# Products of a tile of ones in the planned TensorE gaps of the first batch's attention

## The chip, the cores and the metric
One NeuronCore of one Trainium2 chip runs the whole program. The metric is the time of one execution on the device, in microseconds (us); lower is better. Engines are named as in the profile: PE is TensorE's matmul stream and PEld its weight loads, DVE is VectorE, ACT is ScalarE, POOL is GpSimd, SP issues the transfers. Each engine runs its instructions in the order in which the program gives them, and waits on semaphores where an operand comes from, or a buffer is still read by, another engine.

## What is computed
Attention with rotary embedding over 4 batches, 8 heads, 576 positions and 64 columns a head, and then a gated layer over all 2304 rows:

```python
scores = matmul(rotate(q), rotate(k).T) / sqrt(64)
attn   = exp(scores - max(scores)); attn /= sum(attn) + 1e-9
x      = (attn @ v)  laid out as (2304, 512)
gate   = 1 / (1 + exp(-(x @ w_gate)))            # w_gate, w_val: 512 x 1536
out    = (gate * (x @ w_val)) @ w_out            # w_out: 1536 x 512
```

## The kernel before
**Tiling.** The heads are worked on in 4 pairs (`p`), one head in each half of the 128 partitions. The queries of a pair are split in two halves (`i`) of 256 and 320 columns. The first batch (b = 0) has a path of its own, in fp32. Its generator `front` (lines 626 to 668) makes the scores of a block of 128 queries in one PSUM tile `s` (line 641; the "direct" products) and takes their maximum over the keys on DVE (line 645, a read of both banks of `s`). After the blocks of a half, five short DVE steps (lines 652 to 656) split the maxima in three bf16 parts, PE turns them (line 661), and ACT copies them out (line 668). `back` (lines 670 to 722) then makes the scores the other way round, keys on partitions: products of a tile of ones `onesb` with the negated maxima (line 685) plus the scores (line 690) accumulate in `s`, ACT takes the exponential (line 696), and PE makes the weighted sums `pv` and the row sums `m` (line 707), which DVE divides (lines 717 and 718).

**Beside it.** While batch 0's attention runs, the weights come in: ACT and DVE decode and scale twelve chunks (lines 372 to 400), with a small product per chunk on PE (line 349). From some 93 us on, the gated layer of batch 0 (line 799) begins and PE has work from it between the attention's tasks. Batches 1 to 3 and the last layer (line 833) follow.

**PSUM.** `s_ps` are two tiles of 128 x 2 x 512 fp32, each two banks; the direct products and their readers use columns 0 to 287 of each bank, the others columns 0 to 255 or 319. Columns 384 to 511 of the second bank are written and read by nobody. `v_ps` is one bank, of which the weighted sums use columns 0 to 319 and small maxima (lines 337 to 342) use columns from 384. `m_ps` are three more banks.

**Order.** Every piece of work is a task with an engine, an estimated cost, a rank, and the buffers that it reads and writes. `Plan.order` plays the tasks through with these costs and gives each a planned start; `Plan.emit` then issues the instructions in the order of the planned starts, so each engine's queue has the planner's order. The planner's times decide the order alone: on the chip nothing waits for a planned time. The waits come from the Tile framework, which follows each access to a tile and puts a semaphore wait on the later of two that clash. In PSUM it counts accesses to one bank of a tile as a clash, whatever their columns: in the program of this kernel, the first weighted sums after `values` of a batch (writes of columns 0 to 255 of `pv`) wait for the DVE instruction of line 324 that reads column 384 of that bank and nothing else of `pv`.

Of the kernel before, what the change touches and what calls it, by code (L numbers as in the profile page):

```python
# [35 lines left out]
class Lease:  # L36


    def __init__(self, pool, bufs):
        self.pool, self.bufs, self.users, self.n = pool, bufs, [], None  # L40
# [18 lines left out]
class Plan:  # L59


    HOP = 0.2

    def __init__(self):
        self.tasks, self.preds, self.wrote, self.read = [], [], {}, {}
# [26 lines left out]
    def order(self):  # L92
# [34 lines left out]
        def release(n):  # L127
            for x in self.leases[n]:
                x.left -= 1
                if not x.left:  # L130
                    slots[x.pool][x.n] = max(done[m][1] + done[m][2] for m in x.users) + self.HOP
                    for m in parked.pop(x.pool, []):
                        offer(m)

        def offer(n):
            for e, _ in self.tasks[n][0]:
                t = 0.0
                for m in self.preds[n]:
                    e0, end, land = done[m]
                    t = max(t, end if e0 == e and not land else end + land + self.HOP)  # L140
                heapq.heappush(wait.setdefault(e, []), (t, self.tasks[n][1], n))
# [60 lines left out]

    def emit(self):
        self.starts = self.order()
        for t, n, e in self.starts:
            self.tasks[n][2](e)


# [17 lines left out]
def rope_attention_then_sigmoid_glu(ctx: ExitStack, tc: tile.TileContext, qk, v, w_in, w_out, tables, out):  # L226
    nc = tc.nc
    V, A, G, T, Y = nc.vector, nc.scalar, nc.gpsimd, nc.tensor, nc.sync
# [47 lines left out]
    onesb = sb("onesb", [128, 128], BF16)  # L276
# [4 lines left out]
    s_ps = [psum.tile([128, 2, 512], F32, name=f"s{n}") for n in range(2)]  # L281
# [3 lines left out]
    P = Plan()  # L285
# [628 lines left out]
    for f in range(NF):  # L914
        t = -1.75 + 0.35 * f / NF
        at(t, w_in_chunk, f, t)
    hiddens(0, 0, -1.6, -1.2)
    for f in range(NF):
        t = -1.0 + 0.2 * f / NF
# [14 lines left out]
        projects(b, 1, b + 0.8, b + 1)  # L934
    for _, _, fn, args in sorted(todo):
        fn(*args)
    with tc.manual_schedule():
        P.emit()
    global LAST
# [46 lines left out]
```

## Time and profile before
| | |
|---|---|
| median of 3 runs | 716.72 us (716.29 to 717.3) |
| span of the profiled execution | 719.6 us; its own time is known by this span alone |
| PE busy | 672.3 us (93%), 4986 products |
| DVE busy | 482.9 us (67%) |
| ACT busy | 437.0 us (61%) |
| mean granted TensorE clock | 0.974 of full speed |
| chain that ended last | PE 85%, DVE 8%, ACT 3%, DMA 2% |

Busy times are sums over an engine's instructions. The page also cuts the span into 40 slices of 18 us; the first five or six are the first batch's attention, where PE's busy share is lowest. Idle time of an engine matters only where the chain that ended last runs through it.

### The profile page before, as it was taken

Reading aid. Unit: us, or ns where it says so; the run is one execution under the profiler, and the core shown is the slowest. Engines: PE = TensorE matmul, PEld = TensorE weight load, DVE = VectorE, ACT = ScalarE, POOL = GpSimd, SP = SyncE. Lnnn points to the kernel's source line nnn. Section 1 sums busy time; section 2 is a strip of 40 time slices with the busy share of each in tenths; the row PEclk is TensorE's granted clock in tenths of the full one; section 3 lists DMA queues with packets and bytes.
Section 4 is the critical chain, followed back from the end, with each engine's and each line's share of the span. In section 5 each row is a group of like instructions: output and inputs, shape, how many; then the busy total and the mean of one; then the engine's idle time right before and its main releaser. Section 6 shows DMA issues by size and latency. Waiting matters only on the chain.

```text
span 719.6 us, 12869 instructions
## 1 busy us (share of the span) xinstructions
PE 672.3 (93%) x4986; PEld 426.9 (59%) x4986; DVE 482.9 (67%) x1062; ACT 437.0 (61%) x885; POOL 73.9 (10%) x57
## 2 busy tenths in 40 slices
PE   1687889999999998998998899999999999999997
PEld 1343455565675455775564665578667756866753
DVE  5677676889888668877797886779938682311310
ACT  2583967796878866665776678577738663322320
POOL 0300000000303001133135001114000000000000
PEclk9996989999999999999998999999999999999999
DMA  9731305226364337664996559764544542000001
GB/s 348 315 125 62 133 41 209 93 92 215 122 163 99 96 96 178 161 165 87 203 210 142 105 126 231 166 159 118 126 110 117 90 109 79 1 15 16 1 15 30
DMA packets 145230, 89.38 MB, mean 124 GB/s; under 512 B 128912, under 2 KB 133648, under 8 KB 143248
## 3 DMA queue, kind: packets, MB, share of 16 engines
q1 hardware_dynamic: 145168, 88.56, 45.7%
q8 instruction: 39, 0.64, 0.4%
q14 instruction: 23, 0.19, 0.1%
HBM read 43.12 MB, written 4.72 MB: 66 GB/s over the span
## 4 chain that ended last, share of the span: by engine, by line
PE 85%; DVE 8%; ACT 3%; DMA 2%; issue 1%; SPq 0%; DVEq 0%; ACTq 0%
PE m L799 37%; PE m L833 20%; PE pv L748 6%; PE s L584 5%; PE s L641 3%; PE s L572 3%; PE pv L707 3%; PE s L690 2%; PE m L707 2%; DVE p L366 1%; PE s L685 1%; DVE p L607 1%; DMA stk<-in_qk_dram 1%; DMA pt<-p 1%; DVE m L645 1%
## 5 line engine op out<-in xcount | busy, mean ns | idle before, releaser
L799 PE MATMUL m<-xt,w 128*128 128x320 f16 (+1 forms) x2304 | 297.1, 287 | 2.3 <-ACT th L805 2.3
L799 PEld LDWEIGHTS <-w 128*128 128x128 f16 x2304 | 221.7, 98 | 74.3 <-issue 18.6
L833 PE MATMUL m<-wo,gt 128*128 128x512 f16 x648 | 146.4, 381 | 0.0
L612 ACT ACTIVATE p<-p,st 128x576 f32<-128x576 f32 x108 | 83.1, 770 | 52.0 <-DVE p L607 45.3
L833 PEld LDWEIGHTS <-gt 128*128 128x128 f16 x648 | 62.4, 98 | 74.2 <-issue 5.0
L366 DVE SCALAR_TENSOR_TENSOR p<-p,st,p 128x576 f16<-128x576 f32 x108 | 91.5, 874 | 20.5 <-ACT p L360 20.2
L809 DVE SCALAR_TENSOR_TENSOR th<-th,m 128x256 f32<-128x256 f32 (+1 forms) x96 | 43.1, 450 | 75.1 <-PE m L799 71.9
L360 ACT ACTIVATE p<-p,st 128x576 f16<-128x576 f32 x108 | 78.3, 763 | 10.6 <-DMA pt<-p 4.5
L360 ACT ACTIVATE gt<-th,c_s 128x256 f16<-128x256 f32 (+1 forms) x96 | 50.5, 529 | 55.2 <-DVE th L809 54.9
L366 DVE SCALAR_TENSOR_TENSOR gt<-th,c_s,gt 128x256 f16<-128x256 f32 (+1 forms) x96 | 56.0, 589 | 19.6 <-ACT gt L360 19.4
L805 ACT ACTIVATE th<-m,gsc 128x256 f32<-128x256 f32 (+1 forms) x96 | 47.3, 494 | 35.1 <-PE m L799 34.5
L607 DVE TENSOR_SCALAR_CACHE_REDUCE p<-s,q_e 128x576 f32<-128x576 f32 x72 | 57.2, 811 | 4.7 <-PE s L584 3.9
L748 PE MATMUL pv<-pt,v 128*64 128x256 f16 (+3 forms) x720 | 54.3, 299 | 0.0
L584 PE MATMUL s<-stk 128*128 128x288 f16 (+1 forms) x320 | 44.9, 290 | 6.4 <-DVE p L607 6.4
L641 PE MATMUL s<-stk 64*128 64x288 f32 (+1 forms) x160 | 33.5, 527 | 18.5 <-DVE stk L516 12.3
L523 POOL TENSOR_TENSOR sw<-sw,tab 128x576 f32<-128x576 f32 x16 | 25.7, 1606 | 225.1 <-DMA sw<-in_qk_dram 225.1
L748 PEld LDWEIGHTS <-v 128*64 128x64 f16 (+1 forms) x720 | 37.3, 113 | 17.6 <-issue 12.8
L521 POOL TENSOR_TENSOR qk<-qk,tab 128x576 f32<-128x576 f32 x16 | 22.8, 1446 | 203.9 <-DMA qk<-in_qk_dram 152.2
L584 PEld LDWEIGHTS <-stk 128*128 128x128 f16 (+1 forms) x320 | 27.2, 100 | 20.0 <-issue 11.9
L645 DVE TENSOR_REDUCE m<-s 128x2 f32<-128x576 f32 x36 | 26.9, 753 | 15.1 <-PE s L641 14.7
L360 ACT ACTIVATE o<-m,o_s 128x512 f32<-128x512 f32 x16 | 10.9, 682 | 41.0 <-PE m L833 40.9
L696 ACT ACTIVATE pt<-s 128x512 f32<-128x512 f32 (+3 forms) x40 | 23.8, 601 | 15.5 <-PE s L690 15.3
(122 smaller groups left out, 700.0 us busy)
## 6 DMA issues: line engine op xcount, KB each, us to landing
wo<-in_w_dram SPq DMA_DIRECT2D x12, 1024.0 KB, 4.8
sw<-in_qk_dram SPq DMA_DIRECT2D x16, 576.0 KB, 5.0
xt<-in_wo_dram SPq DMA_DIRECT2D x12, 512.0 KB, 4.5
stk<-in_qk_dram SPq DMA_DIRECT2D x8, 576.0 KB, 5.0
qk<-in_qk_dram SPq DMA_DIRECT2D x8, 576.0 KB, 5.6
out_dram<-o SPq DMA_DIRECT2D x16, 256.0 KB, 2.1
xt<-in_v_dram SPq DMA_DIRECT2D x3, 1152.0 KB, 6.2
stk<-sw SPq DMA_DIRECT2D x16, 216.0 KB, 3.2
```

The lines of the kernel that those rows point to most:

```text
L360: A.activation(o, src, AF.Copy, scale=scale)
L366: V.scalar_tensor_tensor(out=o, in0=src, scalar=scale, in1=hi, op0=ALU.mult, op1=ALU.subtract)
L584: T.matmul(o[:, c, 0:288], lhsT=q[:, rows:rows + width], rhs=kk[:, c * 288:c * 288 + 288], start=(m == 0), stop=(m == 1))
L607: lambda E, h=h, c=c: V.tensor_scalar(out=prs[c]().rearrange("p (c n) -> p c n", c=2), in0=h()[:, :, 0:288], scalar1=down, scalar2=None, o ...
L612: lambda E, c=c: A.activation(prs[c](), prs[c](), AF.Exp, bias=st[:, k, 0, c:c + 1], scale=-1.0, accum_out=st[:, k, 1, c:c + 1]))
L641: T.matmul(o, lhsT=qT[hs, 128 * t:128 * t + w], rhs=kT[hs, 288 * cc:288 * cc + 288], start=True, stop=True)
L707: T.matmul(o[es, 0:n], lhsT=ones[hs, 0:64] if one else v32[hs, p, j if j == 4 else j + 5 * e], rhs=pp[hs, at0:at0 + n], start=(j == 0), st ...
L748: T.matmul(v_ps[64 * e:64 * e + 64, 0:n], lhsT=v16[hs, p, a, g, :], rhs=pt[z][hs, c * 9 + g, 0:n], start=(first and m == 0), stop=(last an ...
L799: T.matmul(m()[:, 0:n], lhsT=w16[:, f, g, a, cc, :], rhs=x[:, cc, c, c0:c0 + n], start=(k == 0), stop=(k == 11))
L805: op("ACT", c_act(n), rank - 0.05, [m, ("gsc", b, f)], [r], lambda E, m=m: A.activation(t(), m()[:, 0:n], AF.Tanh, scale=gsc[:, b, f:f + 1]))
L809: op("DVE", c_dve(n, psum=True), rank - 0.05, [m], [r], lambda E, m=m: V.scalar_tensor_tensor(out=t(), in0=t(), scalar=1.0, in1=m()[:, 0:n ...
L833: T.matmul(m(), lhsT=gt[:, f, a, c0:c0 + 128], rhs=wo16[:, f, c, :], start=(f == 0 and k == 0), stop=(f == NF - 1 and k == 2))
```

## The change
`emit` keeps the planned end `last` of the PE task before. Ahead of each PE task it issues fillers: for a planned gap of g us between two PE tasks, `int((g - 0.3) * 8)` of them, and for the gap ahead of the first PE task, counted from 1.5 us, `int((g - 0.3) * 14)`. From a planned time of 100 us on there are none. A filler is one product of `onesb` with itself (128 x 128 bf16, 128 columns, with a weight load of its own) into columns 384 to 511 of the second bank of `s_ps[0]` or `s_ps[1]`, by turns within a gap, beginning with `s_ps[0]`. Nothing reads these columns. The fillers are not tasks: the planner does not know of them, and the order of all else stays as it was.

```diff
+    FILL = 1.5, 100.0
...
     def emit(self):
         self.starts = self.order()
+        last = self.FILL[0]
         for t, n, e in self.starts:
+            if e == "PE":
+
+                for k in range(int((min(t, self.FILL[1]) - last - 0.3) * (14 if last == self.FILL[0] else 8))):
+                    self.filler(k)
+                last = t + dict(self.tasks[n][0])[e]
             self.tasks[n][2](e)
...
+    P.filler = lambda k: T.matmul(s_ps[k % 2][:, 1, 384:512], lhsT=onesb, rhs=onesb, start=True, stop=True)
     with tc.manual_schedule():
         P.emit()
```

## Rows read from the trace of the kernel before

**Rows 1.** The page's slices of 18 us: granted TensorE clock in tenths

```profile
PEclk9996989999999999999998999999999999999999
```

**Rows 2.** Windows: stretch and its length; busy us (instructions) by engine; granted clock, DMA share, GB/s

```profile
12.30:30.30 18.00, 11.89 (x50) 6.22 (x52) 13.39 (x23) 8.44 (x17) 0.83 (x1) 1.00 1.02 424
...
37.10:40.50 3.40, 3.34 (x18) 1.53 (x16) 1.86 (x6) 2.71 (x6) 0.00 (x0) 0.50 0.17 29
...
57.60:71.30 13.70, 11.23 (x50) 5.90 (x52) 10.21 (x26) 5.43 (x12) 0.00 (x0) 0.50 0.21 78
...
91.70:98.60 6.90, 5.92 (x25) 3.00 (x26) 4.35 (x14) 3.09 (x4) 0.00 (x0) 0.51 0.01 2
...
125.00:700.00 575.00, 564.26 (x4305) 368.84 (x4302) 398.38 (x909) 360.51 (x742) 67.05 (x44) 0.99 0.47 115
```

**Rows 3.** Who PE waited for, 0 to 100 us: total us, times, longest

```profile
PE s L641 <- DVE m L645: 6.2, 5, 2.3
...
PE s L685 <- ACT pt L696: 3.9, 6, 1.0
```

**Rows 4.** Chain of work that ended last, 90 to 101 us: start, us, what

```profile
92.68 2.18 PE s L641 x8
94.86 2.68 PE m L799 x12
...
99.31 1.42 PE m L799 x12
100.73 0.11 PE m L661 x2
```

**Rows 5.** Timeline of POOL, 0.5 to 2 us: start, us, instruction

```profile
0.91 0.20 POOL L854 MEMSET onesb<- 128x128 bf16 x1
```

**Rows 6.** Timeline of PE, 0 to 130 us, with the idle time before and its releaser

```profile
12.29 2.29 PE L641 MATMUL s<-stk 64*128 64x288 f32 x8 [12.29 <-DVE stk L516]
16.89 2.29 PE L641 MATMUL s<-stk 64*128 64x288 f32 x8 [2.31 <-DVE m L645]
19.14 0.59 PE L337 MATMUL pv<-ident,vm 128*1 128x128 f32 x2
...
24.90 0.37 PE L661 MATMUL m<-nid,cb 128*128 128x128 bf16 x2 [3.02 <-DVE cb L656]
...
27.83 1.19 PE L641 MATMUL s<-stk 64*128 64x288 f32 x4
...
53.86 1.24 PE L641 MATMUL s<-stk 64*128 64x288 f32 x8
...
58.33 4.51 PE L641 MATMUL s<-stk 64*128 64x288 f32 x16 [2.03 <-DVE m L645]
63.75 0.39 PE L661 MATMUL m<-nid,cb 128*128 128x128 bf16 x2 [0.91 <-DVE cb L656]
...
68.80 1.12 PE L707 MATMUL pv<-pt,v 128*64 128x256 f32 x4
```

**Rows 7.** Timeline of DVE, 0 to 94 us: reads of the scores

```profile
16.08 1.41 DVE L645 TENSOR_REDUCE m<-s 128x2 f32<-128x576 f32 x2
...
19.22 0.76 DVE L645 TENSOR_REDUCE m<-s 128x2 f32<-128x576 f32 x1
...
24.66 0.75 DVE L645 TENSOR_REDUCE m<-s 128x2 f32<-128x576 f32 x1
...
57.53 1.41 DVE L645 TENSOR_REDUCE m<-s 128x2 f32<-128x576 f32 x2
...
63.60 0.75 DVE L645 TENSOR_REDUCE m<-s 128x2 f32<-128x576 f32 x1
...
91.88 1.41 DVE L645 TENSOR_REDUCE m<-s 128x2 f32<-128x576 f32 x2
```

**Rows 8.** Timeline of ACT, 0 to 70 us: exponentials of the scores

```profile
28.10 0.60 ACT L696 ACTIVATE pt<-s 128x512 f32<-128x512 f32 x1 [0.47 <-PE s L690]
...
68.91 0.60 ACT L696 ACTIVATE pt<-s 128x512 f32<-128x512 f32 x1 [0.47 <-PE s L690]
```

## Prediction
> **What bounds the kernel now.** I read the page's slices first, for the granted clock: it dips in the second to fifth slice, and little afterwards [rows 1]. Windows on the dips place them: 0.50 in 37.1 to 40.5 us, 0.50 in 57.6 to 71.3 and 0.51 in 91.7 to 98.6, the lower of the two levels (1.2 of 2.4 GHz); after 125 us PE is busy 564 of 575 us at 0.99 [rows 2]. So what the opening loses arrives late at a PE that never rests again, and the end moves by as much. The records of the clock begin only at 30 us and show 1.00 before that, but the instructions tell otherwise: eight direct products took 2.29 us at 12.29 and at 16.89, and 1.24 at 53.86 [rows 6]. I count 12.3 to 30.3 us as the lower level too. The waits say what PE idles for in the opening: a DVE maximum read (6.2 us in 5 times) and an ACT exponential (3.9 in 6) [rows 3], each a read of the very `s` tiles into which the fillers go.
>
> **Price of a filler.** Twelve products of 256 columns take 2.68 us at the lower clock and 1.42 at the full one, 0.223 and 0.118 each [rows 4]; half the columns give 0.11 and 0.06. Two products of 128 x 128 bf16 with weights of their own, the filler's form, take 0.11 us on the chain at full clock, 0.056 each [rows 4]. I use c = 0.11 low, 0.056 full. An upper bound of 0.118 at full clock (a weight load sets the pace of the wider pairs) is kept for the range.
>
> **How many, and what they wait for.** The planner's starts, worked through its costs, serve for counts alone: 138 fillers ahead of the first task, then 28, 2, 2, 29, 13, 2, 1, 7, 5, 10, 6, 1, 2, 16, 2, 1, 6, 4, 3, 2, 7, 1, 13, 5, 16, 3; 325 in all. A filler is a write to the second bank of an `s` tile, and by the framework's count by banks it waits for the last earlier-issued read of that tile, though that read touches other columns. Issue order is planned order, so the reads planned inside a gap stand ahead of the gap's fillers. PE takes its queue in order. So in most gaps the first one or two fillers wait until the reads are over, which is when the gap would have ended, or later, since the turn over both tiles also asks for the read of the tile that the next task doesn't need. The rest then run after the gap, ahead of the real work.
>
> No row of this trace tells a bank's columns apart, for every matmul here that waits for a read of `s` also overwrites its columns. The Trainium skill (PSUM — Partial Sum Buffer, Terms) says that TensorE writing a bank while VectorE or ScalarE reads it, in the same quadrant, is an error, without regard to columns, and that a scheduler keeps them apart. By that rule the fillers must wait, and the sum is the one below; by columns alone it would be the first rival's.
>
> **The sum, against the span of 719.6 us.** Delays of PE, in us:
>
> 1. 138 at the start. `onesb` is ready at 1.11 [rows 5]. All low they last 15.2 and end at 16.3; all full, 7.7 and 8.8. The first scores can begin at 12.29 but are first read at 16.08, DVE being busy with the rotation until then [rows 6, 7]. The likely mixture ends near 12. Cost 0; at most 1.4 (16.3 plus half of 2.29, less 16.08).
> 2. 28 ahead of the third score task, which began at 16.89 [rows 6]. The second read ends at 16.08 + 1.41 = 17.49 [rows 7], and some 0.06 pass until PE starts (at most 0.1: half of the two reads is over at 16.79, and PE began at 16.89). So 0.66 + 27c: 2.2 full, 3.6 low. PE sits idle from about 14 to 17.5 for all the fillers; the spell of 0.50 from 57.6 on begins in an idle stretch of 2.03 us [rows 2, 6], so I expect low in most cases: 3.3.
> 3. 2 and 2 around the small maximum: it ran at 19.14 beside the read 19.22 to 19.98 and must now follow it [rows 6, 7]: 0.9 there, 0.7 behind it.
> 4. 29 ahead of the turn at 24.90. DVE reads the last scores of the half at 24.66 to 25.41, after the steps on which the turn waits [rows 6, 7]. So 0.57 + 28c: 2.1 to 3.65; taken 3.3.
> 5. 13 between the turn and the products that wait for ACT's copy of it: 13c is 0.7 to 1.4, of which much lies beside the copy. Cost 0 to 0.8; 0.4.
> 6. 2 ahead of the scores at 27.83, which now wait for an exponential ending at 28.70 [rows 6, 8]: 0.9 in the slow rhythm of before, 0.7 taken.
> 7. 7 behind a DVE read: 7c, 0.6. The 5, 10, 6, 1 and 2 that follow stand behind ACT or DVE reads that end the gap anyway, so each costs about its number less one: 1.1 full; the first is covered by ACT's work on the weights: 0.9.
> 8. 16 at 58.33: the two reads end at 57.53 + 1.41 = 58.94 [rows 6, 7], so 0.67 + 15c: 1.5 to 2.3; 2.1. Then 2, 1 and 6, the last held by the read 63.60 to 64.35 where the turn began at 63.75 [rows 6, 7], 0.66 + 5c = 0.9 to 1.2: with the others 1.4.
> 9. 4, 3 and 2; the 2 make the weighted sums at 68.80 wait for an exponential until 69.51 [rows 6, 8]: 0.9.
> 10. 7, 1, 13 and 5 in a stretch where ACT sets the pace: 1.9 if all showed; 0.3.
> 11. 16 near 90 us meet no read that is still open and fit their gap: 0, or 0.5 at low clock. The last 3 wait until 93.29 for the second read where scores began at 92.68 [rows 4, 7]: 0.8.
>
> Together 8.4 + 1.5 + 3.5 + 0.9 + 0.3 + 0.8 = 15.4. All at full clock it is 11.2, all low with little hidden 21.
>
> Against it stands clock. From low to full a stretch of PE work shrinks by 1 - 1.42 / 2.68 = 0.47. Of 11.89 busy us in 12.3 to 30.3 [rows 2] some 5 lie behind the 29 fillers, which themselves are over 3 us of unbroken work: I credit 1.9 of 2.3. In 57.6 to 71.3 it is 11.23 x 0.47 = 5.3 at most; the first four score tasks are paced by DVE reads of 0.75, and the fillers' own waits leave holes: 2.5. In 91.7 to 98.6, 2.8 at most, and an even chance: 1.4. In 37.1 to 40.5, 1.6 at most; its idle time before stays, so nothing. Credit 5.8.
>
> Net 15.4 - 5.8 = 9.6 us of lengthening. The profiled span is 2.9 above the median of 716.72; the difference is carried to the median: 726.3.
>
> **Rivals.**
>
> *The fillers run in the gaps* (waits by columns alone). What decides is whether fillers are seen between 14 and 16.9 us. For it: the columns are free and the planned density, 8 per us at 0.056, leaves half a gap empty. Against it: the program's own wait between column 384 and columns 0 to 255 of `pv`. Then the whole opening runs at full clock: 2.3 + 1.6 + 5.3 + 2.8 and some 1.5 of the early scores, 13.5 at most; with DVE and ACT pacing parts of it 8: 708.7, on the other side of 716.72. Chance 0.12.
>
> *The fillers wait, but the clock is never lost again*, since what they run after the gaps makes up in density. Cost 11.2, and all the credits, 13.5 less the 1.5 of early scores that the 28 fillers delay anyway: 12. Net -0.8, 716. Against it: PE stays idle 3.5 us ahead of term 2 and again ahead of term 4, longer than before. Chance 0.08.
>
> *The fillers wait, and the clock follows nothing of them*: products of ones might not count as activity, or the new holes undo what the fillers warm. No credit: 15.4, 732. For it: the low spells stand by idle time, which grows. Against it: unbroken PE work brought the full clock back each time. Chance 0.08.
>
> **How the numbers follow.** The likeliest, waits by bank with part of the credit, has 0.72, with its own range 720 to 732 from the terms' ends. 0.2%, or 1.4 us, is about what a measurement of this kernel can tell from no change. Slower by more than that: nearly all of the likeliest, all of the third rival and a little of the second, 0.80. Faster: the first rival and some of the second, 0.14; within, 0.06. The range 715.5 to 732 leaves out the first rival (0.12), half the third, and a little at the top.
>
> **What would show it.** Right: PE idle from about 14 to 17.5 us, then a block of some 27 fillers until 19 to 20.5, the third score task behind it; the same from 25.5 to 27 or 28.5 ahead of the turn; granted clock low while PE waits. The turn at 24.90 before should begin some 7 to 8 us later, and PE after 125 us be as dense as before, shifted by the total. Wrong: fillers inside those gaps, or the first line 799 product earlier than 94.8 us.

## The result, and the profile after

The changed kernel takes 727.06 us (median; 723.99 to 729.73), the kernel before 717.01 on the same chip (716.29 to 718.25): ratio 1.0138, 95% interval 1.0097 to 1.0178, some 10 us slower. Its profiled execution took 729.41 us with a span of 727.6, so 1.8 lie around the span. The four times lie in two groups, 723.99 and 724.71 at a mean granted clock of 0.98, and 729.41 and 729.73 at 0.97, so the median is the middle between the groups and no execution took it. From line 324 to 840 the lines are 8 higher than before: the scores are L649, the maximum's read L653, the turn L661 is L669, the exponential L704, the fillers L946.

The page's head and the slices [rows 1]: PE is busier and the program longer, and the clock is low in two slices from 55 to 91 us, where it was low in one. A stretch at a granted clock of 0.50 is called a low spell below.

```profile
span 727.6 us, 13516 instructions
PE 693.7 (95%) x5311; PEld 448.7 (62%) x5311; DVE 481.8 (66%) x1062; ACT 437.1 (60%) x885; POOL 74.8 (10%) x57
PEclk9797699999999999999998999999999999999999
```

Windows [rows 2] (columns as there): the opening fillers before and after 5.2 us, the first long wait, four low spells, and the stretch behind the opening, where PE is as dense as before.

```profile
1.20:5.20 4.00, 4.00 (x39) 4.00 (x39) 0.00 (x0) 1.33 (x3) 0.64 (x1) 1.00 0.79 276
5.20:11.00 5.80, 5.75 (x102) 5.57 (x100) 3.71 (x3) 0.00 (x0) 0.00 (x0) 1.00 1.00 385
11.40:15.40 4.00, 1.21 (x8) 0.75 (x9) 3.84 (x4) 1.81 (x5) 0.00 (x0) 1.00 1.05 420
15.40:22.20 6.80, 5.62 (x37) 4.19 (x37) 2.26 (x6) 2.43 (x5) 0.00 (x0) 0.50 1.02 429
25.70:32.50 6.80, 3.97 (x38) 3.97 (x38) 2.57 (x7) 0.58 (x2) 2.67 (x2) 0.50 0.87 354
63.20:83.70 20.50, 17.61 (x92) 9.74 (x93) 9.89 (x25) 5.02 (x11) 0.00 (x0) 0.50 0.22 78
107.60:111.00 3.40, 3.40 (x16) 1.97 (x16) 1.79 (x8) 0.59 (x2) 0.00 (x0) 0.50 0.00 0
137.00:700.00 563.00, 555.04 (x4269) 365.28 (x4268) 397.38 (x908) 359.72 (x742) 66.98 (x44) 0.99 0.48 118
```

Who PE waited for, 0 to 112 us [rows 3]. PE still waits for reads of `s` by DVE and ACT, now in 22 waits and 19.5 us, and what stands at the head of its queue is now a filler (the wait for POOL is the one for `onesb` at the start).

```profile
PE s L946 <- DVE m L653: 14.7, 12, 3.7
PE s L946 <- ACT pt L704: 4.8, 10, 0.7
PE s L946 <- POOL m L863: 1.2, 1, 1.2
```

The timeline of PE [rows 6]. One filler starts after the first read of the pair, the other 27 after the second, and the third score task, which started at 16.89, stands behind them at 19.82; the same at 28.53 ahead of the turn, and at 63.98.

```profile
1.17 9.78 PE L946 MATMUL s<-onesb 128*128 128x128 bf16 x138 [1.17 <-POOL m L863]
11.37 1.24 PE L649 MATMUL s<-stk 64*128 64x288 f32 x8 [0.42 <-DVE stk L524]
16.18 0.27 PE L946 MATMUL s<-onesb 128*128 128x128 bf16 x1 [3.57 <-DVE m L653]
16.85 3.04 PE L946 MATMUL s<-onesb 128*128 128x128 bf16 x27 [0.40 <-DVE m L653]
19.82 2.29 PE L649 MATMUL s<-stk 64*128 64x288 f32 x8
...
28.53 3.15 PE L946 MATMUL s<-onesb 128*128 128x128 bf16 x28 [3.67 <-DVE m L653]
31.47 0.42 PE L669 MATMUL m<-nid,cb 128*128 128x128 bf16 x2
...
63.98 1.76 PE L946 MATMUL s<-onesb 128*128 128x128 bf16 x15 [0.40 <-DVE m L653]
65.67 2.29 PE L649 MATMUL s<-stk 64*128 64x288 f32 x8
...
93.52 0.89 PE L946 MATMUL s<-onesb 128*128 128x128 bf16 x13 [0.70 <-ACT pt L704]
```

DVE's reads of the scores [rows 7]: both filler blocks start where a read ends, at 15.38 + 1.41 = 16.79 and 27.73 + 0.75 = 28.48.

```profile
15.38 1.41 DVE L653 TENSOR_REDUCE m<-s 128x2 f32<-128x576 f32 x2
...
27.73 0.75 DVE L653 TENSOR_REDUCE m<-s 128x2 f32<-128x576 f32 x1
```

The chain of waits, 15 to 36 us (start, us, what), where the fillers are now links between DVE's reads and PE's own work.

```profile
15.38 1.43 DVE m L653 x2
16.80 0.04 issue
16.85 3.04 PE s L946 x27
19.89 2.25 PE s L649 x8
...
27.73 0.76 DVE m L653
28.49 0.04 issue
28.53 3.15 PE s L946 x28
31.67 0.21 PE m L669 x2
```

**The shift.** To see where the time comes from I took the start of one PE task after another, counted from the first score task, less the same in the kernel before (us, worked out from the timelines; the first column is the start before). "Again" is a second profile of the changed kernel (720.2 us span); the others are the experiments below. A table entry is one profiled execution less another, not a median.

| task | start before | changed | again | early | two | mid | late | free | free12 |
|---|---|---|---|---|---|---|---|---|---|
| third scores | 16.89 | 3.8 | 3.6 | 3.6 | 0.9 | 0 | 0 | 0 | -0.4 |
| turn | 24.90 | 7.5 | 6.9 | 7.1 | 2.5 | 0 | 0 | -0.6 | -1.7 |
| scores | 31.47 | 7.0 | 5.9 | 5.5 | 4.9 | -0.3 | 0 | -1.9 | -3.0 |
| L349 | 42.84 | 4.8 | 3.6 | 3.0 | 2.6 | 1.5 | 0.3 | 0.7 | 0.1 |
| scores | 53.86 | 5.9 | 4.8 | 3.0 | 3.1 | 1.5 | 0.3 | 0.9 | 0.3 |
| turn | 65.80 | 10.5 | 6.7 | 2.4 | 4.8 | 3.8 | -1.1 | -0.5 | -1.1 |
| L349 | 73.06 | 12.5 | 6.8 | 2.3 | 6.3 | 2.7 | -2.4 | -2.8 | -3.3 |
| L349 | 82.43 | 14.5 | 8.8 | 2.4 | 7.4 | 2.7 | -0.4 | -2.6 | -1.9 |
| L799 | 99.25 | 13.4 | 6.0 | 2.3 | 4.8 | 2.7 | -2.4 | -5.4 | -4.9 |
| L833 | 246.3 | 13.4 | 6.0 | 2.3 | 4.8 | 2.7 | -2.4 | -5.4 | -4.9 |
| L748 | 453 | 8.9 | 0.7 | 1.0 | 1.8 | -1.2 | -7.7 | -9.5 | -10.5 |

From 99 to 246 us nothing changes: what the opening loses is lost. The two profiles of one kernel lose 13.4 and 6.0 there, on either side of the 10.0 between the medians; a profile of the kernel without the 138 loses 13.2. Such a difference can hold a few us that no filler costs. The kernel with the 138 alone shows it: it has no filler behind 12 us, stands within 0.2 us of before up to 54 us, and then at -2.8 at 73.06 and -2.9 at 99.25, though its median isn't below that of before.

Behind 313 us every kernel, the experiments too, loses 1 to 6 us less than the profiled execution of before, whatever its fillers: that one execution had longer waits there, and two low spells (334.1 to 337.5 and 381.9 to 388.7 us) where the changed kernel's profile has one (390.9 to 397.7). Who PE waited for, 313 to 453 us of before:

```profile
PE s L584 <- DVE p L607: 6.4, 5, 2.2
PE m L799 <- ACT th L805: 2.3, 1, 2.3
```

and 323 to 466 us of the changed kernel:

```profile
PE s L592 <- DVE p L615: 4.8, 5, 1.9
PE m L807 <- ACT th L813: 1.2, 1, 1.2
```

So the last row of the table is not to be read as a difference of times: with 1.8 us around its span, as in the changed kernel, the profiled execution of before would have taken an estimated 721.4, above its median.

### The profile page after: what moved, and what is told of

It reads as the page before. It is cut to its first block, busy times and chain, and to the rows that moved or that the text cites. A ratio compares the mean times of both kernels' runs of the same rounds, so it can differ in the third digit from the quotient of the medians.

```text
span 727.6 us, 13516 instructions
## 1 busy us (share of the span) xinstructions
PE 693.7 (95%) x5311; PEld 448.7 (62%) x5311; DVE 481.8 (66%) x1062; ACT 437.1 (60%) x885; POOL 74.8 (10%) x57
## 4 chain that ended last, share of the span: by engine, by line
PE 87%; DVE 7%; ACT 3%; DMA 1%; issue 1%; SPq 0%; DVEq 0%; ACTq 0%
PE m L807 38%; PE m L841 19%; PE pv L756 7%; PE s L592 5%; PE s L580 3%; PE s L649 3%; PE pv L715 3%; PE s L698 3%; PE m L715 2%; PE s L946 2%; DVE p L374 1%; DMA sw<-in_qk_dram 1%; DVE m L653 1%; PE s L693 1%; DVE p L615 1%
## 5 line engine op out<-in xcount | busy, mean ns | idle before, releaser
L374 DVE SCALAR_TENSOR_TENSOR gt<-th,c_s,gt 128x256 f16<-128x256 f32 (+1 forms) x96 | 58.7, 616 | 19.5 <-ACT gt L368 19.2
L946 PE MATMUL s<-onesb 128*128 128x128 bf16 x325 | 31.9, 256 | 20.7 <-DVE m L653 14.7
L946 PEld LDWEIGHTS <-onesb 128*128 128x128 bf16 x325 | 26.0, 118 | 28.1 <-issue 26.7
L653 DVE TENSOR_REDUCE m<-s 128x2 f32<-128x576 f32 x36 | 26.9, 754 | 21.1 <-PE s L649 19.7
L704 ACT ACTIVATE pt<-s 128x512 f32<-128x512 f32 (+3 forms) x40 | 23.7, 601 | 18.3 <-PE s L698 18.1
```

Of the source, the lines that this page charges most:

```text
L374: V.scalar_tensor_tensor(out=o, in0=src, scalar=scale, in1=hi, op0=ALU.mult, op1=ALU.subtract)
L946: P.filler = lambda k: T.matmul(s_ps[k % 2][:, 1, 384:512], lhsT=onesb, rhs=onesb, start=True, stop=True)
```

## The experiments

The theory (A): fillers wait for the open reads of their bank, what is behind the waits delays PE's own work, and some is given back as clock. Each experiment is a change to the changed kernel; "before" was timed beside it.

**Only the 138 at the start, and all but these.** First:

```diff
-    FILL = 1.5, 100.0
+    FILL = 1.5, 12.0
```

> Only the 138 fillers ahead of the first task stay. Theory A (fillers wait for reads of their bank, and what they run after the gaps is the loss): these 138 meet no read, end near 11 us and cost nothing; their clock is gone again before the second scores. 716 to 718.5, same as before. Rival B (the loss comes from the head: the first scores start late, or PE's queue is clogged): 722 to 728.

718.47 us against 717.78 (ratio 1.001, 0.9991 to 1.0028). Then their factor is set to 0, and the 187 others stay:

```diff
-                for k in range(int((min(t, self.FILL[1]) - last - 0.3) * (14 if last == self.FILL[0] else 8))):
+                for k in range(int((min(t, self.FILL[1]) - last - 0.3) * (0 if last == self.FILL[0] else 8))):
```

> The 138 are left out, the other 187 stay. Theory A: all of the loss stays, 725 to 731. Rival B (the head): 716 to 719.

727.43 us against 717.78 (1.0134, 1.0085 to 1.0184). The 138 cost nothing and bring nothing that can be measured; the 187 are the whole change.

**At most two in each later gap.** The waits stay, the work behind them goes.

```diff
-                for k in range(int((min(t, self.FILL[1]) - last - 0.3) * (14 if last == self.FILL[0] else 8))):
+                for k in range(min(2 if last > self.FILL[0] else 999, int((min(t, self.FILL[1]) - last - 0.3) * (14 if last == self.FILL[0] else 8)))):
```

> The 138 stay, every other gap gets two fillers at most, one to each tile: the waits stay, the work behind them goes. Theory A, with its own terms: waits of 0.6 + 0.7 + 0.6 + 0.7 + 0.7 + 0.7 + 0.8 + 0.7 us and little work are some 5 us, less what ACT or DVE hide: 719 to 723, the clock as before. Rival C (the wait for the other tile is the whole loss): 726 to 729. Rival D (only the filler's work counts): 716 to 718.

723.56 us against 717.78 (1.0088, 1.0058 to 1.0118): half a us above the range expected. With the waits and next to no work behind them the kernel is 5.8 us slower than before, and 3.9 faster than with all of the 187 (727.43, above). The intervals of these two overlap, so how the 10 us divide between waits and work is only roughly known. On the timeline the third scores are 0.9 us late, not 3.8:

```profile
16.73 0.27 PE L946 MATMUL s<-onesb 128*128 128x128 bf16 x1 [3.35 <-DVE m L653]
17.39 0.26 PE L946 MATMUL s<-onesb 128*128 128x128 bf16 x1 [0.40 <-DVE m L653]
17.59 2.29 PE L649 MATMUL s<-stk 64*128 64x288 f32 x8
```

**The same 325 fillers, into banks that nothing reads just then.** `opened` holds for each bank the planned end of its last access; a gap's fillers go to the bank with the earliest. The banks are the second ones of both `s` tiles, the three of `m`, and `pv` (64 columns free there, so a product of 64). After the first gap a filler adds to what stands in its columns.

```diff
+                count = int((min(t, self.FILL[1]) - last - 0.3) * (14 if last == self.FILL[0] else 8))
+                at = min(opened, key=opened.get)
...
-                    self.filler(k)
+                    self.filler([*self.banks][k % 6] if last == self.FILL[0] else at, last == self.FILL[0])
...
+            else:
+                for x in self.uses[n]:
...
+                        opened[at] = max(opened[at], self.done[n][1])
...
+    P.filler = lambda at, new: T.matmul(P.banks[at], lhsT=onesb, rhs=onesb[:, 0:P.banks[at].shape[1]], start=new, stop=new, ...
```

> Same number of fillers in the same places of PE's order, but each gap's go to the PSUM bank whose last read was planned to end earliest (spare columns of s, m or pv; 64 columns wide in pv), so that none has a wait of its own. Theory A: they run inside the gaps and the clock holds: 706 to 713, faster than before. Rival E (fillers cost their own time wherever they run, or don't hold the clock): 717 to 727.

711.52 us against 717.78: 0.9913, 0.9884 to 0.9942, so faster than before by 6.3. The timeline (lines are 16 higher than before): the fillers now run in the gaps, where PE waited in both other kernels, and the third scores wait for DVE alone. Of the waits from 0 to 112 us a single one is a filler's, the one for `onesb` at the start:

```profile
PE s L956 <- POOL m L871: 1.2, 1, 1.2
```

The start of two gaps:

```profile
12.58 0.99 PE L956 MATMUL pv<-onesb 128*128 128x64 bf16 x28
16.00 1.42 PE L657 MATMUL s<-stk 64*128 64x288 f32 x8 [2.44 <-DVE m L661]
...
20.30 3.27 PE L956 MATMUL m<-onesb 128*128 128x128 bf16 x29
23.40 0.39 PE L677 MATMUL m<-nid,cb 128*128 128x128 bf16 x2
```

A window of it, columns as in [rows 2]: two low spells stand ahead of it (17.5 to 24.3 and 34.5 to 41.4 us), but none is left between 41.4 and 95 us, where before has the one from 57.6 to 71.3 and the first half of the one from 91.7.

```profile
41.40:95.00 53.60, 47.62 (x431) 28.20 (x429) 42.13 (x84) 37.49 (x74) 0.00 (x0) 1.00 0.31 107
```

The same number of products, in the same gaps, costs 10 us where it meets open reads and gains 6 where it doesn't. The wait is the cause. Two more things differ, products of 64 columns in `pv` and products that add in place of overwriting; the next kernel does without the first and gains as much, and the second wasn't tried alone. Whether a filler waits by the bank or by the whole tile `s` of two banks no run tells, for every read that held one covers both banks.

How much of the 6.3 us comes from the opening's clock is less clear: at 99.25 this profile stands 5.4 us ahead of that of before but 2.5 ahead of the one with the 138 alone, and another 4 come behind 282 us, where no filler stands.

**12 per planned us, in free banks.** As the last, with 12 fillers per us of planned gap in place of 8, and without `pv`, so that all are 128 columns wide.

```diff
-                count = int((min(t, self.FILL[1]) - last - 0.3) * (14 if last == self.FILL[0] else 8))
+                count = int((min(t, self.FILL[1]) - last - 0.3) * (14 if last == self.FILL[0] else 12))
```

> As the version whose fillers go to the bank with no open read, but 12 per planned us in place of 8, all of them 128 columns wide (banks of s and m, none in pv). Theory A: the gap ahead of the third score task, in which the clock still fell with 28 narrow fillers, stays at full clock, and the opening gains more: 706 to 711. Rival G (what the fillers can give is given; more of them overrun their gaps): 712 to 717.

710.49 us against 719.77: 0.9887, 0.9852 to 0.9922. This beats the kernel before and the changed kernel, and is the version to keep; that it beats the 8 per us isn't shown, for the intervals overlap. Its windows: from 11.3 to 95 us a single low spell, 36.8 to 40.2 us, where before has three [rows 2], and a fourth by the pace of its first products [rows 6].

```profile
11.30:36.70 25.40, 19.70 (x215) 13.35 (x214) 20.91 (x35) 14.46 (x28) 6.46 (x4) 1.00 0.80 329
36.80:40.20 3.40, 3.40 (x17) 1.66 (x16) 1.87 (x3) 2.43 (x3) 0.00 (x0) 0.50 0.40 106
40.20:95.00 54.80, 51.58 (x489) 31.82 (x487) 42.26 (x83) 37.52 (x73) 0.00 (x0) 1.00 0.32 112
```

**16 per planned us.** The same with `else 16`.

> The version with fillers in banks without open reads at 16 per planned us. Theory A: at full clock 16 fillers take 0.9 of a planned us and still fit, the clock has one low spell less, 707 to 710. Rival G (overrun): 711 to 714.

715.16 us against 718.85: 0.9953, 0.9932 to 0.9973. It gives back more than half of the gain, and is slower than either theory had it. The fillers of the first gap now end where DVE releases the scores (12.24 + 3.36 = 15.60), and a low spell of 6.8 us stands at 35.8:

```profile
12.24 3.36 PE L956 MATMUL m<-onesb 128*128 128x128 bf16 x57
15.66 1.42 PE L657 MATMUL s<-stk 64*128 64x288 f32 x8
```

```profile
35.80:42.60 6.80, 5.97 (x28) 2.75 (x30) 3.21 (x7) 2.44 (x5) 0.11 (x1) 0.50 0.44 154
```

That the density past 12 gains nothing is shown; whether the little overrun or the other place of the spell makes it slower is not. In these two profiles little of the difference lies in the opening: the shift (as in the table) is -3.7 here against -4.9 with 12 at 99.25, and -6.7 against -10.5 at 453.

**Which gap costs what: early, middle, late.** Three kernels with the 138 and a part of the rest. Early (28, 2, 2, 29; `FILL = 1.5, 24.2`):

> The changed kernel with fillers up to the turn at 24.9 us of before only: 138, 28, 2, 2 and 29; the other 126 left out. Theory A: these places hold 0.7 + 3.3 + 3.3 = 7.3 us of delay, and the block of 29 gives back up to 2.3 of clock behind it: 721 to 724. Rival F (the loss is spread evenly over all places, 61 of 187 blocked fillers a third of it): 719 to 721.

718.02 us against 719.77 (0.9992, 0.9966 to 1.0019): no difference, and a miss for the theory, which had added the terms' costs. Its profile, of the slowest of its ten executions (722.36 us), does show the terms, 7.1 us late at the turn. But 4.1 of it is given back by 42.84, and it stands 2.3 late at the end of the opening.

Middle (2, 16, 2, 1, 6, 4, 3, 2, planned for 54 to 67 us):

```diff
-            if e == "PE":
+            if e == "PE" and (last == self.FILL[0] or 54.0 < t < 67.0):
...
+            if e == "PE":
                 last = t + dict(self.tasks[n][0])[e]
```

> The changed kernel with the 138 and the fillers planned from 54 to 67 us only (2, 16, 2, 1, 6, 4, 3, 2). The shift of PE's tasks in the two profiles of the changed kernel grew by 6.6 and 2.0 us over this stretch. Theory A (blocked fillers there delay, and the low spell from 58 us on is lengthened or shortened by them, execution by execution): 719 to 724, with a shift of 2 to 6 us at the first line 799 product of the trace. Rival H (only together with the earlier fillers): 716 to 718.

721.26 us against 718.85 (1.0028, 1.0001 to 1.0055), barely clear of no change, and in the range that the theory gave. Late (7, 1, 13, 5; the same with `70.0 < t < 82.0`):

> The 138 and the fillers planned from 70 to 82 us only (7, 1, 13, 5). Theory A as it was predicted (ACT's work on the weights covers them): 716 to 718, a shift under 0.5 us in the trace. Rival I (nothing covers them; both profiles of the changed kernel grew by 2.0 here): 718 to 720, a shift of about 2 us.

715.91 us against 718.85 (0.9962, 0.9945 to 0.9978): faster, which neither theory gave. The four gaps themselves cost what the rival said, 2.0 us (-2.4 to -0.4 in the table). The chain of waits there shows the fillers as links behind ACT's exponentials (lines are 9 higher than before here):

```profile
79.11 0.55 ACT pt L705
79.66 0.04 issue
79.70 0.89 PE s L947 x13
80.59 0.21 PE s L694 x2
```

Against the profile of the kernel with the 138 alone, this one lacks a low spell at 81.2 to 84.6 us. That makes up for the 2.0 us and no more: at 99.25 it stands at -2.4, the other at -2.9. It gets ahead behind 282 us (-7.7 against -3.9 at 453), where neither has fillers. So the profiles don't show the 2.9 us as a gain of these fillers, and why the median is lower stays open.

By their ratios the three parts come to -0.6, +2.0 and -2.7 us and the whole to +10. They hold 123 of the 187 fillers; the 45 between the turn and 54 us and the 19 near 90 are in none of them. In the two profiles of the changed kernel these two stretches add nothing (the shift falls by 1.6 and 2.1 us from the turn to 53.86, and by 1.2 and 2.8 from 82.43 to 99.25), so it is likely, but not shown, that the costs of the places don't add, because where the low spells fall depends on all of them. The changed kernel itself, profiled once more:

> The changed kernel once more, for a second profile of it. Its runs so far lie near 724 and near 729.5 with a mean granted clock of 0.981 and 0.966. Theory A: the blocks of fillers stand in the same places whatever the time, and the two differ by where the low spells fall: at 724 one of the spells of the opening is shorter.

721.99 us, span 720.2, on a chip on which before took 719.77. The long low spell of the changed kernel, 20.5 us from 63.2, is here one of 6.9 from 69.1; the two windows of it are

```profile
63.20:69.10 5.90, 4.21 (x36) 2.51 (x35) 4.30 (x12) 0.00 (x0) 0.00 (x0) 1.00 0.01 3
69.10:76.00 6.90, 5.81 (x35) 3.52 (x35) 4.43 (x12) 2.61 (x6) 0.00 (x0) 0.51 0.41 152
```

and between the tasks at 53.86 and 82.43 us it lost 4.0 us where the other lost 8.6. Program and waits are the same; what differs in these windows is the clock.

## Why the prediction was right, and where it was right by luck

The direction, the mechanism and the total held: +9.6 forecast, +10.0 measured. That the total came so near is in part luck: the forecast of 726.3 us lies between the two groups of times, and no execution of the four came within 1.5 us of it. By its steps (us of shift added, from the timelines; step 3 is read at the scores that began at 20.04):

| step | predicted | changed | again |
|---|---|---|---|
| 1, the 138 | 0 | 0 | 0 |
| 2, 28 ahead of the third scores | 3.3 | 3.8 | 3.6 |
| 3, 2 and 2 | 0.7 | 0.7 | 0.3 |
| 4, 29 ahead of the turn | 3.3 | 3.0 | 2.9 |
| from the turn to 31.47: terms 5, 6 less the credit 1.9 | -0.8 | -0.5 | -1.0 |
| 31.47 to 42.84, part of 7 | +0.6 | -2.2 | -2.2 |
| 42.84 to 53.86, the rest of 7 | +0.9 | +1.1 | +1.1 |
| 53.86 to 65.80, term 8 | +3.5 | +4.6 | +1.9 |
| 65.80 to 73.06, term 9 less the credit 2.5 | -1.6 | +2.1 | +0.1 |
| 73.06 to 82.43, term 10 | +0.3 | +2.0 | +2.0 |
| 82.43 to 99.25, term 11 less the credit 1.4 | -0.6 | -1.2 | -2.8 |

**What held.** Steps 2 to 4 were the first read's end plus so many fillers by their price, and came within half a us: the 27 lasted 3.04 us (0.113 each), the 28 ahead of the turn 3.15 (0.113), as "low in most cases" had it. The reads that hold them were the ones named. "The fillers wait by bank" stood on one wait between two column ranges of `pv` and is shown twice, as against a wait by columns: by the waits of L946, and by the free banks, where they are gone. The Trainium skill (PSUM — Partial Sum Buffer, Terms) speaks of the bank and not of columns. The trace agrees in that the program waits for DVE's reads of other columns of the bank, 14.7 us in 12 waits; what the chip would do without these waits no run here shows.

**What failed.** The mis-sized terms are the credits and term 10.

- The credit for 57.6 to 71.3 ("2.5") came in one profile and not in the other. From 53.86 to 73.06 the sum has +1.9 in all (terms 8 and 9 less the credit). "Again" shows +2.0, its spell being 6.9 us long; the changed kernel shows +6.6, its spell being 20.5. The sum credited a spell with what fillers next to it would release; the runs show that the spells move, to 63.2 or 69.1, with the same program.
- In 31.47 to 42.84 the sum gave nothing for the spell 37.1 to 40.5 ("its idle time before stays, so nothing"). Both profiles lack it, and 2.2 us are given back.
- Term 10 ("0.3", with ACT taken to set the pace, 1.9 if all showed) is 2.0 in both profiles and with these fillers alone (late): the fillers stand between an exponential and the product whose result the next exponential reads, on the chain that ACT paces, so ACT doesn't cover them but waits for them.

The errors, +4.7 or +0.1 from 53.86 to 73.06 and +1.7 in term 10 against -2.8 at 31.47 to 42.84 and -0.6 or -2.2 behind 82.43, cancel to a good part. The total was nearer than its parts deserved, and the early experiment says the same: 7.1 us of delay at the turn, none of it in the time.

**The rivals.** The first one's mechanism (fillers in the gaps) is not this kernel's, but its price was near: made so by other banks, the kernel is 6.3 us faster than before and, denser, 9.3, where it said 8. The second ("the clock is never lost again", 716) is ruled out by the time and by the low spells behind 15.4 us; the third (no credit, 732) lies above all four times.

**What stays open.** What each gap's fillers cost for themselves, and why some executions draw the long spell at 63 us. The Trainium skill (TensorE: Matmul & The Clock Gate, What's actually happening) says that the watch over PE's activity runs free and doesn't begin with the kernel; that fits with two profiles of one program whose spells fall differently, but no run here shows it.

## What to carry to other kernels

A product that nobody reads is free only if its bank is: put fillers where no other engine has an open read in the queue, or they hold PE past the gap that they were to fill, and then run on the path. Place them by bank, not by column, and count what stands behind them in PE's queue. Where clock and waits are both at stake, sum up the waits from the timeline, but leave a credit for the clock as a range, and take more than one profile before reading a few us into one.

## What the runs showed of the hardware

- Products of ones with ones count as work for the clock: the 39 opening fillers in the window up to 5.2 us took 4.00 us (0.103 each) and the 102 in the next window, three of them in both, 5.75 (0.056), though no other work ran on PE, and the eight scores behind them took 1.24 us, where before they took 2.29. The profile writes 1.00 for both windows; ahead of the first clock record the pace of the instructions has to be read instead.
- PE idled for 3.57 us behind its scores in the changed kernel, until 16.18; the granted clock is 1.00 from 11.4 to 15.4 us and 0.50 from 15.4 to 22.2.
- A run of fillers costs 0.056 to 0.06 us each at the full clock (42 in 2.52) and 0.113 at the lower one (28 in 3.15), about twice as much.
- Four executions of the changed kernel on one chip lie between 723.99 and 729.73 us. Two profiles of it, of 729.41 and 721.99 us on two chips, differ by 7.4 us in span and by as much at 99.25, at the end of the opening, where their low spells fall differently (20.5 us from 63.2, 6.9 from 69.1).
